# A retention layer and its gated feed-forward: order of the first loads, and the down-projection of the first chunk in thirds

## The chip, the cores and the metric

The kernel runs on one core of a Trainium2 chip. A time is that of the device for one execution, in microseconds (us); the figure for a kernel is the median of its runs.

## The reference, cut to what matters

Inputs are q, k, v of shape (4 batches, 8 heads, 768 positions, 64) and the feed-forward weights, all float32. The output has 3072 rows of 512.

```python
for t in range(S):                                   # S = 768, per batch and head
    state = gamma * state + outer(k[t], v[t])        # gamma = 1 - 2 ** (-5 - head)
    y[t] = scale * (q[t] @ state)
x = y.transpose(0, 2, 1, 3).reshape(B * S, H * D)    # 3072 x 512
xn = x / sqrt(mean(x * x) + 1e-6) * rms_g
out = (silu(xn @ w_gate) * (xn @ w_val)) @ w_out     # 512 -> 1536 -> 512
```

## The kernel before, in words

**Tiling.** The recurrence is computed in six chunks of 128 positions. Within a chunk, scores of q and k are taken on PE, masked by decay on DVE and multiplied with v; earlier chunks enter through a 64 x 64 state per head. The decay is folded into scalings of v and of the result. After that a chunk's 512 rows (4 batches x 128) are normed, transposed and put through the feed-forward: `gv` multiplies blocks of 128 gate and value columns (12 blocks) and leaves silu(gate) * value in `hT`; `down` multiplies `hT` with wo, 12 matmuls of 128x512 for each batch. Chunks 0 and 1 are worked in pairs of batches (pair 0: batches 0 and 1; pair 1: batches 2 and 3) with 64 partitions for each batch. In chunks 0 and 1 PE transposes q and k (`tp`, copied out by `tc_`), and chunk 0's masks hold the decay itself.

**Order.** The program is written out by hand: each engine carries out its instructions in the order of the text, from L568 on, and engines wait for one another by semaphores alone. What matters here is the head of the text, up to the first chunk's feed-forward, and three queues in it:

- POOL issues all transfers that convert float32 to bf16 (q, k and weights), and some of v. Its order: q and k of pair 0 (L124, L132), the index patterns `off` and `offp`, half of v of pair 0 (L136), q and k of pair 1 (L137, L138), the positions `pos_p`, `pos_n`, the exponents `ya_p` (L195), weight blocks 0 to 4 two at a time (L569, L570; `load_w` L83 is one transfer of wg and one of wv), the power for pair 0's norm (L603), blocks 4 to 8, the scaling of v (`vp_pair`), blocks 8 to 10, the power for pair 1 (L633), loads of chunk 1, blocks 10 to 12, wo in three parts (L652).
- SP issues the other half of v of pair 0 (L119) and, after the first masked score, v of pair 1 (L587).
- PE alternates pair 0's work, pair 1's transposes and scores, and `gv` blocks of pair 0 (columns 0 to 256 of the chunk), then pair 1's `y0`, its norm and transposes (`x_pe`, L644), then the rest of `gv`. `heat(n)` is n matmuls of ones whose result nobody reads.

The norm of chunk 0 (`squares0`, `eps0`, `power`, `norm0`) runs over ACT, DVE and POOL. `v_cast` (L267) makes a bf16 copy of v on ACT; `y0` needs it. `exponents` (L198) makes `va_p` and `va_n` on DVE from `pos_p` and `pos_n`.

**PSUM.** `bank` (L65) hands out the eight banks. First the list `first` (L59), then the cycle `order`; once `split[0]` is set, attention takes banks 0 to 3 in turn and the feed-forward 4 to 7. A new tile in a bank waits until the readers of the old one are through. Before, `split[0]` is set at L723, ahead of chunk 1's feed-forward.

**The first down-projection** (L682 to L709): `down(0, 0)` stands behind `y1(0)`, chunk 1's values of pair 0; `down(0, 1)` and `down(0, 2)` follow pair 0's norm; then come the transposes and scores of chunk 1, pair 1 (`tp`, `x_pe` of pair 0, `ap`), and `down(0, 3)`. Each copies its result to `o_sb` (three buffers) on ACT and stores it from SP's queue, on which the transposing loads of chunk 2 (`t_dma`) are queued too.

Of the kernel before, what the change touches and what calls it, by code (L numbers as in the profile page):

```python
# [8 lines left out]
F32 = mybir.dt.float32  # L9
# [7 lines left out]
def kernel(  # L17
# [11 lines left out]
    nc = tc.nc  # L29
    ctx.enter_context(tc.manual_schedule())  # L30

    B, H, S, D = q.shape
    C = 128
    NCH = S // C
    NHP = H // 2
    DM = H * D
    DFF = moe_w_gate.shape[1]
    KS = DM // 128
    NFF = DFF // 128
# [5 lines left out]
    work = ctx.enter_context(tc.tile_pool(name="work", bufs=4))  # L45
# [17 lines left out]
    split = [False]  # L63

    def bank(name, dtype=F32, ffn=False, i=None):  # L65
        if i is None and split[0]:
            i = turn[ffn] % 4 + 4 * ffn
            turn[ffn] += 1
        elif i is None and first:
            i = first.pop(0)  # L70
        elif i is None:
            i = order[0]
            order.append(order.pop(0))
        return psum.tile([128, 512 if dtype == F32 else 1024], dtype, name=name, tag=f"p{i}")
# [3 lines left out]
    wo_b = const.tile([128, NFF, DM], BF16, name="wo_b")  # L78
# [4 lines left out]
    def load_w(n0, n1, *kinds):  # L83
        sl = slice(n0 * 128, n1 * 128)
        for i in kinds or (0, 1):
            nc.gpsimd.dma_start(out=(wg_b, wv_b)[i][:, :, sl], in_=(wg_v, wv_v)[i][:, :, sl])
# [4 lines left out]
    U = {}  # L91

    def load_pair(c, p, n, batches=(0, 1), eng=None, after=None):
        u = U.setdefault((c, p), {})
        if n not in u:
            if n == "v":
                u[n] = work.tile([128, H, 2 * D], F32, name="v2f", bufs=3)
            else:
                u[n] = work.tile([128, H, 2 * D], BF16, name=n + "2b", bufs=4)
        for b in batches:  # L100
            i = (eng or nc.gpsimd).dma_start(out=u[n][b * 64:b * 64 + 64], in_=pair_v[n][c, 2 * p + b])  # L101
            if after is not None:
                tc.add_manual_dep(i.ins, after.ins.name, SYNC_DEP, reason="transfer order")
# [30 lines left out]
    for i in range(2):  # L134
        nc.gpsimd.iota(offp[i * 64:i * 64 + 64], pattern=[[-1, 2], [1, 2], [2, 64]], base=0, channel_multiplier=-2)
    load_pair(0, 0, "v", (1,))  # L136
    load_pair(0, 1, "q")  # L137
    load_pair(0, 1, "k")  # L138
    for i in range(2):
        nc.gpsimd.iota(pos_p[i * 64:i * 64 + 64], pattern=[[C, 2], [1, 2]], base=1, channel_multiplier=2,  # L140
                       allow_small_or_imprecise_dtypes=True)
# [36 lines left out]
    def mask_exp(a):  # L178
        for i in range(2):
            for x in range(2):  # L180
                nc.scalar.activation(mask0[a][i][:, x], reach, AF.Exp, scale=lng[2 * (2 * a + x) + i], bias=lnscale)
# [11 lines left out]
    for e in range(2):  # L193
        r = slice(e * 64, e * 64 + 64)
        nc.gpsimd.tensor_tensor(out=ya_p[r], in0=pos_p[r, 1, e:e + 1].to_broadcast([64, H]),  # L195
                                in1=lngs[r], op=ALU.mult)

    def exponents():  # L198
        nc.vector.tensor_tensor(
            out=va_p, in0=pos_p[:, :, None, :].to_broadcast([128, 2, H, 2]),  # L200
            in1=lngs[:, None, :, None].to_broadcast([128, 2, H, 2]), op=ALU.mult)
        nc.vector.tensor_tensor(
            out=va_n, in0=pos_n[:, :, None].to_broadcast([128, NCH, H]),
            in1=lngs[:, None, :].to_broadcast([128, NCH, H]), op=ALU.mult)
# [11 lines left out]
    def heat(n, i=7):  # L216
        hot = bank("hot", i=i)
        for _ in range(n):
            nc.tensor.matmul(hot, ones[:, :128], ones, start=True, stop=True)  # L219

    def copy(eng, out, in_):
        return (nc.scalar.copy if eng == "a" else nc.vector.tensor_copy)(out, in_)


    def tp(c, p, n, a, eng=None):

        u = U[c, p]
        ps = bank("t_ps", BF16)
        view = ps[:, :512].rearrange("p (x b e j) -> p x e b j", x=2, b=2, e=2)
        for x in range(2):  # L230
            for e in range(2):
                for i in range(2):
                    h = 2 * (2 * a + x) + i
                    nc.tensor.transpose(view[i * 64:i * 64 + 64, x, e], u[n][:, h, e * D:e * D + D], ident)  # L234
        u["t_ps", n, a] = ps
        if eng:
            tc_(c, p, n, a, eng)

    def tc_(c, p, n, a, eng):
        u = U[c, p]  # L240
        t = work.tile([128, 2, 2, 2, 64], BF16, name=n + "2T", tag=n + "T", bufs=8)
        copy(eng, t.rearrange("p x b e j -> p (x b e j)"), u["t_ps", n, a][:, :512])
        u[n + "T", a] = t
# [14 lines left out]
    def ap_mask(c, p, a, i):  # L258
        u = U[c, p]
        am = work.tile([128, 2, 2, 128], BF16, name="am2", tag="am", bufs=12)  # L260
        m = mask0[a][i] if c == 0 else causal_p[:, None, :].to_broadcast([128, 2, 256])
        u["mask", a, i] = nc.vector.tensor_tensor(  # L262
            out=am.rearrange("p x e t -> p x (e t)"),
            in0=u["a_ps", a][i].rearrange("p (x t) -> p x t", x=2), in1=m, op=ALU.mult)
        u["am", a, i] = am

    def v_cast(p):  # L267
        u = U[0, p]
        u["vb"] = work.tile([128, H, 2 * D], BF16, name="vb", bufs=2)
        nc.scalar.copy(u["vb"], u["v"])  # L270
# [87 lines left out]
    def begin(c):  # L358
        XT[c] = work.tile([128, KS, GT], BF16, name="xnT", bufs=2)
# [35 lines left out]
    def y1_out(p):  # L395
        u = U[1, p]
        x = work.tile([128, 2, NHP, 2, D], F32, name="x", tag="x", bufs=2)
        u["x"] = x.rearrange("p b a i d -> p b (a i d)")
        for b in range(2):
            nc.vector.tensor_tensor(  # L400
                out=u["x"][:, b].rearrange("p (h d) -> p h d", h=H), in0=u["y"][b].rearrange("p (h d) -> p h d", h=H),
                in1=yd_p[:, :, None].to_broadcast([128, H, D]), op=ALU.mult)
# [115 lines left out]
    HT = {}  # L518
# [22 lines left out]
    def store(eng, c, b, m, o_sb):  # L541
        if c < 2:
            for e in range(2):
                eng.dma_start(out=out_e[c, b, e][:, m], in_=o_sb[e * 64:e * 64 + 64, m])
        else:
            eng.dma_start(out=out_v[c, b][:, m], in_=o_sb[:, m])

    def down(c, b):
        ps = bank("o_ps", ffn=True)
        for n in range(NFF):  # L550
            nc.tensor.matmul(ps, HT[c][:, n, b * C:(b + 1) * C], wo_b[:, n, :], start=n == 0, stop=n == NFF - 1)  # L551
        o_sb = work.tile([128, DM], F32, name="o_sb", bufs=3)
        nc.scalar.copy(o_sb, ps)  # L553
        store(nc.sync, c, b, slice(0, DM), o_sb)

    def down_last(c, b):
        o_sb = work.tile([128, DM], F32, name="o_sb", bufs=3)
        for i in range(2):
            m = slice(i * 256, i * 256 + 256)
            ps = bank("o_ps", ffn=True)  # L560
            for n in range(NFF):
                nc.tensor.matmul(ps[:, :256], HT[c][:, n, b * C:(b + 1) * C], wo_b[:, n, m],  # L562
                                 start=n == 0, stop=n == NFF - 1)
            copy("av"[i], o_sb[:, m], ps[:, :256])
            store(nc.scalar if i == 0 else nc.sync, c, b, m, o_sb)


    begin(0)  # L568
    load_w(0, 2)  # L569
    load_w(2, 4)  # L570

    mask_exp(0)
    mask_exp(1)
    heat(11)
    tp(0, 0, "q", 0, "v")
    tp(0, 0, "q", 1, "v")
    heat(1)
    tp(0, 0, "k", 0, "v")
    tp(0, 0, "k", 1, "v")
    exponents()  # L580
    heat(2)
    ap(0, 0, 0)
    ap(0, 0, 1)
    for a in range(2):
        for i in range(2):
            ap_mask(0, 0, a, i)
    load_pair(0, 1, "v", eng=nc.sync, after=U[0, 0]["mask", 0, 0])  # L587
    v_cast(0)

    g_ps = bank("g_bc_ps")  # L590
# [6 lines left out]
    squares0(0)  # L597
    tp(0, 1, "q", 0, "a")
    tp(0, 1, "q", 1, "a")
    tp(0, 1, "k", 0)  # L600
    tp(0, 1, "k", 1)
    eps0(0)
    power(0, 0)  # L603
    tc_(0, 1, "k", 0, "v")
    tc_(0, 1, "k", 1, "v")
    load_w(4, 6)
    load_w(6, 8)
    vp_pair(0, 0)
# [70 lines left out]
    gv(0, 11, 12, 0, GT)  # L679
    load(2, 0)  # L680
    y1(0)
    down(0, 0)  # L682
    y1_out(0)
    square(1, 0, 0)
    square(1, 0, 1)
# [3 lines left out]
    load(2, 1)  # L689
    vp_pair(1, 1)  # L690
    load(2, 2)
    down(0, 1)
    down(0, 2)
    t_dma(2, 0)
    for n, e in (("q", "a"), ("k", "v")):
        for a in range(2):
# [9 lines left out]
            ap_mask(1, 1, a, i)  # L706
    load(2, 3)
    t_dma(2, 1)
    down(0, 3)  # L709

    def run(steps, after):
        for i, step in enumerate(steps):
# [4 lines left out]
    def L(f, *a):  # L717
        return lambda: f(*a)
# [1 line left out]

    steps = [L(gv, 1, n, n + 2, t, t + 256) for t in (0, 256) for n in range(0, NFF, 2)]
    steps += [L(down, 1, b) for b in range(B)]
    split[0] = True  # L723
    run(steps, {
        0: [L(y1, 1), L(y1_out, 1), L(kvp, 1, 1)],
        1: [L(square, 1, 1, 0), L(square, 1, 1, 1), L(rstd, 1, 1), L(state1, 1)],
# [18 lines left out]
    for c in range(2, NCH):  # L745
# [6 lines left out]
        after = {}  # L752
        if d < NCH:
            after = {
                0: [L(begin, d)],
                1: [L(values, d, 0), L(vp, d, 2), L(vp, d, 3)],
                2: [L(y_out, d, 0, 0)] + [L(load, d + 1, 0)] * more,
                3: [L(y_out, d, 0, 1)] + [L(state_add, d, 0)] * more,
                4: [L(square, d, 0, 0)] + [L(load, d + 1, 1)] * more,
                5: [L(a_pair, d, 1), L(a_mask, d, 2, 0), L(square, d, 0, 1), L(rstd, d, 0)]  # L760
                   + [L(state_cast, 0)] * more,
                6: [L(a_mask, d, 2, 1), L(norm, d, 0, 0), L(x_dma, d, 0, 0)]
# [40 lines left out]
```

## Time and profile before

| | us |
|---|---|
| median of 11 runs | 239.38 (238.43 to 241.1) |
| the profiled execution | 240.46 |
| its span in the profile | 238.7 |
| PE busy | 225.7 (95%) |
| DVE, POOL, ACT busy | 129.2, 115.7, 87.5 |

The profile is of one execution. "Busy" is time in which an instruction of the engine ran; PE's weight loads (PEld) overlap its matmuls. A row of a timeline has the start in the span, the length, the engine, the line, the operation, its tiles and shapes, the number of instructions merged, and in brackets the idle time before it with what ended it. The row of a stretch has its length and then, for PE, PEld, DVE, ACT and POOL, busy time and number of instructions; at its end stand the granted PE clock (1.00 is full), the share of the transfer engines and GB/s. The chain is followed back from the last instruction to whatever released each step; a row has start, length and the step.

### The profile page before, as it was taken

The page shows a single profiled execution, that of the slowest core. Times are in us where ns is not written, and L with a number is a line of the kernel's source. Part 1 is how long each engine was busy: PE and PEld are TensorE (multiplying, and loading weights), DVE is VectorE, ACT ScalarE, POOL GpSimd, SP SyncE. Part 2 cuts the span into 40 slices and gives each one's busy share as a digit, 9 for nine tenths or more (in the row PEclk, how much of TensorE's full clock was granted, in tenths as well). Part 3 has the DMA queues.
Part 4 walks back from the last instruction along what each step waited for, and adds up shares of the span by engine and source line. Part 5 has one row for each costly group of instructions (what it writes and reads, how often), then busy time and mean ns, then how long its engine had stood idle before and what let it go on. Part 6 is the DMA issues. An engine that isn't in the chain of part 4 may idle for free.

```text
span 238.7 us, 5411 instructions
## 1 busy us (share of the span) xinstructions
PE 225.7 (95%) x2198; PEld 137.3 (58%) x2223; DVE 129.2 (54%) x222; ACT 87.5 (37%) x176; POOL 115.7 (48%) x150
## 2 busy tenths in 40 slices
PE   6785999999999999999999999999999999999993
PEld 2453785545788865585454684444674444854443
DVE  3774735638676585837866346966245742243300
ACT  2954544333153244225424235323325241333221
POOL 8966599839869941981936902927001000000000
PEclk9999999999999999999999999999999999999999
DMA  8999999999999999599999993994510204200022
GB/s 106 162 190 200 152 165 162 195 205 201 189 145 178 199 160 175 102 179 132 89 133 179 103 174 124 110 190 109 156 56 0 44 3 141 79 3 0 0 88 89
DMA packets 83306, 30.24 MB, mean 127 GB/s; under 512 B 69521, under 2 KB 78993, under 8 KB 83282
## 3 DMA queue, kind: packets, MB, share of 16 engines
q0 software_dynamic: 51328, 16.52, 64.2%
q1 hardware_dynamic: 31280, 13.25, 27.7%
q8 instruction: 17, 0.28, 0.5%
q10 hardware_dynamic: 674, 0.14, 0.3%
q14 instruction: 7, 0.06, 0.1%
HBM read 28.32 MB, written 6.29 MB: 145 GB/s over the span
## 4 chain that ended last, share of the span: by engine, by line
PE 86%; DMA 6%; DVE 3%; POOL 2%; issue 2%; DVEq 0%; POOLq 0%
PE v_ps L532 25%; PE o_ps L551 25%; PE g_ps L532 24%; DMA wv_b<-in_moe_w_val_dram 4%; DMA k2b<-in_k_dram 2%; PE y_ps L505 2%; PE a_ps L460 2%; DVE am L262 1%; PE y_ps L489 1%; PE t_ps L234 1%; PE o_ps L562 1%; PE kv_ps L498 1%; PE a_ps L255 1%; PE x_ps L365 1%; POOL q2b L101 1%
## 5 line engine op out<-in xcount | busy, mean ns | idle before, releaser
L537 DVE TENSOR_TENSOR hT<-sg,v_ps 128x512 bf16<-128x512 bf16 (+1 forms) x76 | 49.8, 656 | 75.3 <-PE v_ps L532 72.9
L532 PE MATMUL v_ps<-xnT,wv_b 128*128 128x256 bf16 (+1 forms) x427 | 74.9, 309 | 2.3 <-DMA wv_b<-in_moe_w_val_dram 1.9
L532 PE MATMUL g_ps<-xnT,wg_b 128*128 128x256 bf16 (+1 forms) x415 | 73.5, 307 | 1.7 <-DMA wg_b<-in_moe_w_gate_dram 1.0
L536 ACT ACTIVATE sg<-g_ps 128x512 bf16<-128x512 f32 (+1 forms) x76 | 43.7, 574 | 81.8 <-PE g_ps L532 76.9
L551 PE MATMUL o_ps<-wo_b,hT 128*128 128x512 bf16 x268 | 60.8, 379 | 0.4
L532 PEld LDWEIGHTS <-wv_b 128*128 128x128 bf16 x428 | 41.6, 98 | 23.4 <-DMA wv_b<-in_moe_w_val_dram 2.8
L532 PEld LDWEIGHTS <-wg_b 128*128 128x128 bf16 x428 | 40.3, 98 | 21.2 <-DMA wg_b<-in_moe_w_gate_dram 1.3
L551 PEld LDWEIGHTS <-hT 128*128 128x128 bf16 x276 | 26.5, 98 | 31.4
L429 POOL TENSOR_SCALAR m<-ms 128x2 f32<-128x2 f32 x10 | 2.2, 219 | 68.8 <-ACT xsq L424 68.8
L553 ACT COPY o_sb<-o_ps 128x512 f32<-128x512 f32 x23 | 13.4, 582 | 43.7 <-PE o_ps L551 43.7
L437 DVE SCALAR_TENSOR_TENSOR xn<-x,rstd,g_bc 128x512 bf16<-128x512 f32 x20 | 21.9, 1122 | 12.9 <-POOL rstd L345 12.9
L469 DVE TENSOR_TENSOR am<-a_ps,causal 128x512 bf16<-128x512 f32 x32 | 20.8, 678 | 0.0
L443 POOL TENSOR_TENSOR vp<-v_f,vd_n 128x512 bf16<-128x512 f32 x16 | 20.1, 1277 | 0.0
L113 POOL DMA_DIRECT2D qb<-in_q_dram x16 | 15.0, 937 | 0.6 <-DMA wo_b<-in_moe_w_out_dram 0.6
L424 ACT ACTIVATE xsq<-x 128x512 bf16<-128x512 f32 x20 | 12.4, 623 | 7.7 <-DVE x L415 7.7
L113 POOL DMA_DIRECT2D kb<-in_k_dram x16 | 14.3, 896 | 1.8 <-DMA wo_b<-in_moe_w_out_dram 1.8
L110 POOL DMA_DIRECT2D v_f<-in_v_dram x16 | 14.7, 917 | 0.0
L415 DVE TENSOR_TENSOR x<-y_ps,yd_n 128x512 f32<-128x512 f32 x16 | 10.8, 682 | 0.6 <-PE y_ps L505 0.6
L219 PE MATMUL hot<-ones 128*128 128x512 bf16 x22 | 7.8, 457 | 1.5 <-DVE ones L146 1.4
L275 POOL TENSOR_TENSOR vp<-v2f,vd_p 128x1024 bf16<-128x1024 f32 x4 | 7.8, 1945 | 0.1
L345 POOL TENSOR_TENSOR rstd<-m,mhalf 128x2 f32<-128x2 f32 x10 | 7.2, 718 | 0.8
L101 POOL DMA_DIRECT2D q2b<-in_q_dram x8 | 5.8, 738 | 0.8 <-POOLq L787 0.8
(92 smaller groups left out, 154.6 us busy)
## 6 DMA issues: line engine op xcount, KB each, us to landing
v_f<-in_v_dram POOLq DMA_DIRECT2D x16, 256.0 KB, 7.7
out_dram<-o_sb SPq DMA_DIRECT2D x15, 256.0 KB, 2.3
out_dram<-o_sb SPq DMA_DIRECT2D x17, 128.0 KB, 4.4
qb<-in_q_dram POOLq DMA_DIRECT2D x16, 128.0 KB, 6.0
kb<-in_k_dram POOLq DMA_DIRECT2D x16, 128.0 KB, 7.2
wg_b<-in_moe_w_gate_dram POOLq DMA_DIRECT2D x6, 256.0 KB, 9.3
wv_b<-in_moe_w_val_dram POOLq DMA_DIRECT2D x6, 256.0 KB, 10.0
wo_b<-in_moe_w_out_dram POOLq DMA_DIRECT2D x3, 512.0 KB, 9.4
```

What stands on the lines that cost most here:

```text
L110: nc.gpsimd.dma_start(out=x, in_=unit_v[n][c, b])
L113: nc.gpsimd.dma_start(out=x.rearrange("p (h d) -> p h d", h=H), in_=unit_v[n][c, b])
L415: nc.vector.tensor_tensor(out=x[:, :, :, i, :], in0=u["y"][i].rearrange("p (b a d) -> p b a d", b=2, a=NHP), in1=yd_n[:, c, i][:, None, :, ...
L424: nc.scalar.activation(xsq, u["x"][:, b], AF.Square, scale=1.0 / math.sqrt(DM), accum_out=u["ms_"][:, b:b + 1])
L437: nc.vector.scalar_tensor_tensor(out=u["xn"][b], in0=u["x"][:, b], scalar=u["rstd"][:, b:b + 1], in1=g_bc, op0=ALU.mult, op1=ALU.mult)
L443: nc.gpsimd.tensor_tensor(out=x, in0=U[c, b]["v"], in1=vd_n[:, c, :, None].to_broadcast([128, H, D]), op=ALU.mult)
L469: nc.vector.tensor_tensor(out=x, in0=u["a_ps"][i].rearrange("p (a t) -> p a t", a=NHP), in1=causal[:, None, :].to_broadcast([128, NHP, 128 ...
L532: nc.tensor.matmul(x[:, o:o + w], wt[:, s, n * 128:(n + 1) * 128], XT[c][:, s, t0:t1], start=s == 0, stop=s == KS - 1)
L536: nc.scalar.activation(sg[:, :m], ps[0][:, :m], AF.Silu)
L537: return nc.vector.tensor_tensor(out=HT[c][:, n0:n1, t0:t1], in0=sg[:, :m].rearrange("p (n t) -> p n t", t=w), in1=ps[1][:, :m].rearrange( ...
L551: nc.tensor.matmul(ps, HT[c][:, n, b * C:(b + 1) * C], wo_b[:, n, :], start=n == 0, stop=n == NFF - 1)
L553: nc.scalar.copy(o_sb, ps)
```

## The change

Four edits, all of order. Weight block 0 alone is loaded ahead of pair 1's q and k, which move behind the positions and `ya_p`; block 1 and blocks 2 to 4 follow them. The load of v of pair 1 moves from SP's queue to POOL's, behind the first power. `exponents` moves ahead of the copies of the first k, one of pair 1's k copies goes from DVE to ACT, and the counts of `heat` change. The first chunk's down-projection is done in thirds of wo, for all four batches in turn, in four banks held at once, and `split[0]` is set ahead of it.

```diff
     load_pair(0, 0, "v", (1,))
-    load_pair(0, 1, "q")
-    load_pair(0, 1, "k")
+    load_w(0, 1)
     for i in range(2):
         nc.gpsimd.iota(pos_p[i * 64:i * 64 + 64], pattern=[[C, 2], [1, 2]], base=1, channel_multiplier=2,
...
                                 in1=lngs[r], op=ALU.mult)
+    load_pair(0, 1, "q")
+    load_pair(0, 1, "k")
+    load_w(1, 2)
+    load_w(2, 4)
...
+    DP = {}
+
+    def down_third(c, t, *bs):
+
+        for b in bs or range(B):
+            if t == 0:
+                DP[b] = bank("o_ps", ffn=True)
+            for n in range(4 * t, 4 * t + 4):
+                nc.tensor.matmul(DP[b], HT[c][:, n, b * C:(b + 1) * C], wo_b[:, n, :], start=n == 0, stop=n == NFF - 1)
+            if t == 2:
+                o_sb = work.tile([128, DM], F32, name="o_sb", bufs=3)
+                nc.scalar.copy(o_sb, DP[b])
+                store(nc.sync, c, b, slice(0, DM), o_sb)
...
     begin(0)
-    load_w(0, 2)
-    load_w(2, 4)
-
     mask_exp(0)
     mask_exp(1)
-    heat(11)
+    heat(12)
     tp(0, 0, "q", 0, "v")
     tp(0, 0, "q", 1, "v")
-    heat(1)
+    exponents()
+    heat(3)
     tp(0, 0, "k", 0, "v")
     tp(0, 0, "k", 1, "v")
-    exponents()
     heat(2)
...
-    load_pair(0, 1, "v", eng=nc.sync, after=U[0, 0]["mask", 0, 0])
     v_cast(0)
...
     tp(0, 1, "q", 1, "a")
+    heat(3)
     tp(0, 1, "k", 0)
     tp(0, 1, "k", 1)
     eps0(0)
     power(0, 0)
     tc_(0, 1, "k", 0, "v")
-    tc_(0, 1, "k", 1, "v")
+    tc_(0, 1, "k", 1, "a")
+    load_pair(0, 1, "v")
     load_w(4, 6)
     load_w(6, 8)
...
     y1(0)
-    down(0, 0)
+    split[0] = True
+    down_third(0, 0)
     y1_out(0)
...
-    down(0, 1)
-    down(0, 2)
+    down_third(0, 1)
+    down_third(0, 2, 0)
     t_dma(2, 0)
...
-    down(0, 3)
+    down_third(0, 2, 1, 2, 3)
...
     steps += [L(down, 1, b) for b in range(B)]
-    split[0] = True
```

## The prediction

> **What bounds the kernel now.** I read the page first: PE is busy 225.7 of 238.7 us, and of its forty slices only the first four and the last show less than 9 tenths. So I asked for the busy time by stretches.
>
> ```profile
> PE   6785999999999999999999999999999999999993
> ...
> 17.48:28.45 10.97, 7.85 (x115) 5.34 (x116) 6.50 (x15) 5.76 (x11) 5.98 (x8) 1.00 1.35 189
> 28.45:48.50 20.05, 19.79 (x278) 13.42 (x281) 10.50 (x20) 8.19 (x17) 18.14 (x23) 1.00 1.20 168
> 48.50:61.40 12.90, 12.76 (x121) 6.48 (x121) 8.54 (x13) 3.97 (x9) 9.82 (x12) 1.00 1.71 219
> ```
>
> First number after the stretch: its length; then PE's busy time. From 28.45 on PE idles 0.3 us in 20 and 0.1 in 13: what comes later moves one for one with the head, unless the change opens gaps there. Between the first feed-forward (gv) matmul (17.48) and the transposes of the second pair's normed rows (x_pe, 28.45) PE idles 3.1 us. PE's timeline of that stretch says why:
>
> ```profile
> 18.95 0.61 PE L532 MATMUL v_ps<-xnT,wv_b 128*128 128x256 bf16 x4 [0.88 <-DMA wv_b<-in_moe_w_val_dram]
> ...
> 21.45 0.61 PE L532 MATMUL g_ps<-xnT,wg_b 128*128 128x256 bf16 x4 [1.01 <-DMA wg_b<-in_moe_w_gate_dram]
> 23.11 0.61 PE L532 MATMUL v_ps<-xnT,wv_b 128*128 128x256 bf16 x4 [1.05 <-DMA wv_b<-in_moe_w_val_dram]
> ...
> 24.53 0.64 PE L290 MATMUL y_ps<-vb,am 64*128 64x64 bf16 x32
> ...
> 25.78 0.61 PE L532 MATMUL v_ps<-xnT,wv_b 128*128 128x256 bf16 x4
> ```
>
> Three waits for weights, 2.94 us. The chain agrees: one 9.60 us transfer fills it before 25.78.
>
> ```profile
> 15.41 0.73 POOL wg_b L86
> 16.14 9.60 DMA wv_b<-in_moe_w_val_dram
> ```
>
> Last, issue plus landing time, one transfer at a time (v2f, wg_b, wv_b, q2b, k2b in short windows). Second pair: q lands at 10.1 and 11.0, k at 11.8 and 12.5. Weights by two blocks (256 KB each): 14.8, 18.9, 21.4, 23.1, 24.4, 25.7, 27.1, 28.4. From 23.1 on the step is 1.34 us, before it up to 4.1. In between lies that pair's v (2 x 256 KB, from SP's queue): issued at 10.86 and 11.52, landed at 19.7 and 22.2, and ACT's cast of it ran at 22.32. So the stage is bound by transfers, and mixing the two queues is its slow part.
>
> **The change part by part.** *First block and POOL's queue.* A half block (128 KB, 256-byte rows) has its nearest row in q and k: 128 KB in 256-byte rows land every 0.75 to 0.87 us, against 0.67 for half of a 1.34 us step. Four halves cost 4 x 0.13 = 0.5 us of transfer (ends 0.3 and 0.8) and two more issues of 0.76 on POOL. POOL after its v issue (5.92): two halves to 7.45, iotas and the yield exponents 1.0 to 8.45, q and k (four of 0.69) to 11.2, four weight issues to 14.25. The power waits for DVE until 14.69 today: cover 0.44 us; without it each further issue would add 0.76 to the first norm.
>
> *Exponents.* DVE now waits for pos_n (about 8.1), 0.28 of work, done at 8.4; behind it queue the copies of kT, which start at 8.95 for k landed at 8.36. Cost nothing; cover 0.5.
>
> *Heat matmuls.* 12 for 11 lie ahead of a 0.95 wait, 3 for 1 ahead of a 1.23 wait; at 0.43 and 2 x 0.22 they fit. The new three before the second k's transposes lie in that k's wait, below.
>
> *Second q, k.* Issue to landing was 4.2 to 4.6 with this queue ahead, so q (issued 8.45 and 9.15) lands at 12.6 and 13.3, k at 14.0 and 14.7 to 15.0: 2.3 later. PE is in order: tp of k at 14.75 (13.43 before), its copies to 15.4 (DVE) and 15.95 (ACT, 0.53; this one now ahead of the first norm on ACT, 15.44 before), scores (ap) 16.05 to 16.7, heat 0.2, the first x_pe at 16.9 (16.18), first gv at 18.2 (17.48). Loss 0.7 (ends 0.4 and 1.1), covered if the next item ends later.
>
> *Second v on POOL's queue.* Here a rule speaks against the change. Issued at 10.86 from SP, v took 8.9 and 10.7 us; the first pair's second half, POOL-issued, took 4.2, landing 1.04 after the k before it. The Trainium skill, "DMA: Bandwidth & Descriptors", section "Issuing engine by pattern", has simple loads go from Sync and calls that path generally faster. By the rule, v from POOL would not land before today's 22.2, and POOL's two issues (1.4 us) would be pure cost; the head would gain nothing. By the rows I take another sum: once k has landed (14.7), halves 0.8 each: 15.5, 16.3; blocks of 1.34: 17.65, 19.0; v at 1.2 each, between 1.04 and the 1.35 of the next chunk's: 20.2, 21.5. Bound below: issue 16.1 + 4.2 = 20.3. Bound above: the rate of 14.8 to 22.2, 1 MB in 7.45 us = 141 KB/us, for everything after 14.7 (1.31 MB in 9.3): 24.0. I take 21.5, since the slow rate ends when SP's transfers end.
>
> *What is late next.* Weights no longer hold gv 0 to 3 (18.2 to 21.7). Then the cast of v: 21.5 + 1.05 = 22.6, so y0 of pair 1 starts at 22.65 (24.53). The cast stands on ACT ahead of two Silus, DVE's hT behind those and bn_stats behind hT: bn at 22.6 + 0.4 + 2 x 0.42 = 23.85 (25.24), x_pe 3.2 later as today: 27.05. The other arm: v_ps of block 4 needs its block, 1.34 x 2 after v, 24.2 (25.78), x_pe 2.67 later: 26.9. The head gains 28.45 - 27.05 = **1.4 us**; with v at 20.3 it gains 2.6, at 24.0 it loses 1.1. vp_pair and later loads on POOL shift by 1.4 for the two v issues and sat 5 us before the second power: hidden.
>
> *Down-projection by thirds.* As many matmuls (48) and copies. The last wo third lands at 49.1, wanted at 50.2 today; with loads and PE both moved up, the thirds save nothing (at most 0.3 of PE's gain). Their price is the banks: four are held, and `split` leaves four to attention. Today:
>
> ```profile
> 56.34 0.64 PE L234 MATMUL t_ps<-ident,q2b 128*64 128x128 bf16 x16
> 56.81 0.61 PE L234 MATMUL t_ps<-ident,k2b 128*64 128x128 bf16 x16
> 57.35 0.83 PE L365 MATMUL x_ps<-ident,xn 128*128 128x128 bf16 x8
> 58.12 0.75 PE L255 MATMUL a_ps<-q2T,k2T 64*64 64x128 bf16 x32
> 58.80 2.76 PE L551 MATMUL o_ps<-wo_b,hT 128*128 128x512 bf16 x11
> ```
>
> From the first transpose to the next o_ps: 2.46 us. In the new order the first x_pe takes the bank of the first transposed q, which ACT frees after the o_sb copy (0.58) and its own (0.53): 1.3 after the start instead of 1.0; the second x_pe waits for the next copy (1.85), and the second scores for DVE's copy of x_ps (2.75). Sum 3.05: **+0.6 us** (ends 0 and 0.9). Stores of three batches move behind the chunk-2 transposes on SP; these start earlier for it, and nothing waits for a store but the fourth o_sb.
>
> **Sum.** -1.4 + 0.6 = -0.8. The profiled execution took 240.46 (span 238.7 and 1.8 around it): 239.7. The median of the runs is 1.1 below it: 239.38 - 0.8 = 238.6.
>
> **Rivals.** *Rates stay mixed* (the other side): v queued behind six weight transfers moves at 141 KB/us whichever queue it is in. It lands at 24.0, head +1.1, banks +0.6: 241.1. It breaks even at v = 22.4 and decides for slower by 0.5% at 23.6. For it: the step from 14.8 to 18.9. Against: 1.34 us steps right after, and v from POOL at 1.04. *All of the head*: v lands near its bound (20.3 to 20.8) and bank waits hide behind the transposes' own: 2.1 to 2.6 less 0 to 0.3, 237.1. For it: PE's own work would allow y0 at 21.7. Against: four weight transfers are ahead. *Does nothing*: the wait on weights turns into one on v's cast or on k, of the same length; head 0, banks 0 to 0.6: 239.7. The profile excludes it only if v lands before 22.
>
> **How the numbers follow.** Measurement tells 0.5% (1.2 us) from no change. Forecast 0.48, its own range 237.9 to 239.3; all of the head 0.27; nothing 0.08; mixed rates 0.17. Faster by over 0.5% (below 238.2): all of the head and a fourth of the forecast, 0.39. Slower (above 240.6): most of mixed rates, 0.15. Within: 0.46. Range 236.9 to 240.5: it leaves out most of mixed rates and the tail of the second case.
>
> **What would show it.** Right: no PE wait on wg_b or wv_b in blocks 0 to 3; q and k transposes of pair 1 up to 1.3 us later, first gv near 18.2; v landed near 21.5, cast at once, and PE waiting about 0.9 us ahead of y0 for it; x_pe of pair 1 near 27.05; 3.0 us from tp(1,1) to the next o_ps, with waits by ACT and DVE copies. Wrong: v landed after 22.4; the first power on POOL starting after 14.7, because issues took over 0.76; a wait on wo_b inside the thirds; or new PE gaps after the thirds, where I count none.

## The result, and the profile after

The changed kernel takes 243.08 us (median of 12 runs, 241.08 to 249.9), the kernel before 239.41 in the 47 runs made beside it. The ratio is 1.0117, with a 95% interval of 1.0089 to 1.0144: slower by 2.1 to 3.4 us, above the forecast of 238.6 and above the range, which ended at 240.5. Runs that a disturbance of the chip lengthened are in the medians here, and out of every ratio.

The profiled execution took 241.38 us, with a span of 239.2; 2.2 us lie outside the span, where before's had 1.8 (the means over all runs are 2.11 and 1.78). Its busy tenths and its stretches, cut at the same places as those of before (length, then busy time and number of instructions of PE, PEld, DVE, ACT and POOL, granted clock, share of the transfer engines, GB/s):

```profile
PE   7777899999999999999999999999999999999993
...
17.48:28.45 10.97, 8.79 (x147) 6.50 (x137) 7.09 (x16) 6.31 (x13) 7.43 (x10) 1.00 1.37 203
28.45:48.50 20.05, 19.79 (x278) 13.43 (x281) 10.65 (x20) 8.19 (x17) 18.23 (x23) 1.00 1.26 178
48.50:61.40 12.90, 12.31 (x116) 6.38 (x118) 7.14 (x13) 3.70 (x9) 11.58 (x14) 1.00 1.65 191
```

From 17.48 to 28.45 PE is busier by 0.9 us, 28.45 to 48.50 is unchanged, and the stretch with the down-projection has lost 0.45 us. PE's timeline of the changed kernel's head:

```profile
13.75 0.64 PE L237 MATMUL t_ps<-ident,q2b 128*64 128x128 bf16 x16 [0.60 <-DMA q2b<-in_q_dram]
...
15.78 0.64 PE L237 MATMUL t_ps<-ident,k2b 128*64 128x128 bf16 x16 [0.65 <-DMA k2b<-in_k_dram]
...
19.19 0.60 PE L535 MATMUL g_ps<-xnT,wg_b 128*128 128x256 bf16 x4 [0.24 <-ACT xnT L225]
...
24.40 0.64 PE L293 MATMUL y_ps<-vb,am 64*128 64x64 bf16 x32 [1.56 <-ACT vb L273]
...
25.42 0.60 PE L535 MATMUL v_ps<-xnT,wv_b 128*128 128x256 bf16 x4
...
28.35 0.65 PE L368 MATMUL x_ps<-ident,xn 128*128 128x128 bf16 x8 [0.32 <-ACT xn L355]
```

No wait on weights is left in blocks 0 to 3. One wait of 1.56 us for v's cast stands in its place, and the second pair's x_pe comes at 28.35, against 28.45 in the profile of before. By these two profiles alone the head has gained a tenth of a microsecond. The chain of the changed kernel says what fills it:

```profile
15.53 0.69 POOL v2f L101
16.22 7.07 DMA v2f<-in_v_dram
23.28 0.02 issue
23.31 1.04 ACT vb L273
```

And PE's timeline around the thirds, with the waits that the prediction announced: 3.20 us from the first transpose to the next o_ps (2.46 before, 3.05 predicted).

```profile
56.27 0.64 PE L237 MATMUL t_ps<-ident,q2b 128*64 128x128 bf16 x16
56.74 0.61 PE L237 MATMUL t_ps<-ident,k2b 128*64 128x128 bf16 x16
...
57.51 0.87 PE L368 MATMUL x_ps<-ident,xn 128*128 128x128 bf16 x8
58.31 1.00 PE L258 MATMUL a_ps<-q2T,k2T 64*64 64x128 bf16 x32
...
59.47 0.81 PE L567 MATMUL o_ps<-wo_b,hT 128*128 128x512 bf16 x3 [0.16 <-issue]
```

The waits are those: x_pe starts when ACT has copied the first transposed q, and the second scores when DVE has copied x_ps. So the two traces show 0.1 us gained in the head and 0.7 lost at the banks (3.20 less 2.46), and not where 2.8 us come from.

### The profile page after: what moved, and what is told of

It reads as the page before. It is cut to its first block, busy times and chain, and to the rows that moved or that the text cites. A ratio compares the mean times of both kernels' runs of the same rounds, so it can differ in the third digit from the quotient of the medians.

```text
span 239.2 us, 5420 instructions
## 1 busy us (share of the span) xinstructions
PE 226.6 (95%) x2204; PEld 138.3 (58%) x2229; DVE 127.7 (53%) x221; ACT 88.1 (37%) x177; POOL 118.6 (50%) x154
## 4 chain that ended last, share of the span: by engine, by line
PE 84%; DMA 5%; DVE 4%; POOL 2%; issue 2%; ACT 2%; DVEq 0%; POOLq 0%
PE v_ps L535 25%; PE g_ps L535 24%; PE o_ps L554 21%; PE o_ps L567 4%; DMA v2f<-in_v_dram 3%; DMA k2b<-in_k_dram 2%; PE y_ps L508 2%; PE a_ps L463 2%; DVE am L265 1%; PE y_ps L492 1%; PE o_ps L579 1%; PE kv_ps L501 1%; DVE hT L540 1%; PE t_ps L237 1%; POOL q2b L101 1%
## 5 line engine op out<-in xcount | busy, mean ns | idle before, releaser
L440 DVE SCALAR_TENSOR_TENSOR xn<-x,rstd,g_bc 128x512 bf16<-128x512 f32 x20 | 20.2, 1038 | 11.2 <-POOL rstd L348 11.2
L556 ACT COPY o_sb<-o_ps 128x512 f32<-128x512 f32 x19 | 11.0, 581 | 33.0 <-PE o_ps L554 33.0
L110 POOL DMA_DIRECT2D v_f<-in_v_dram x16 | 14.7, 919 | 0.0
L222 PE MATMUL hot<-ones 128*128 128x512 bf16 x28 | 9.4, 444 | 1.5 <-DVE ones L145 1.4
```

The costliest lines, as they stand in the source:

```text
L110: nc.gpsimd.dma_start(out=x, in_=unit_v[n][c, b])
L440: nc.vector.scalar_tensor_tensor(out=u["xn"][b], in0=u["x"][:, b], scalar=u["rstd"][:, b:b + 1], in1=g_bc, op0=ALU.mult, op1=ALU.mult)
```

## The experiments

**The theories.** *Clock* (A in the expectations): many runs of the changed kernel show a granted clock below 1.00, so gaps in the new head cost PE its clock. *Thirds* (B): the banks account for all of it. *Bytes* (C): up to x_pe of the second pair the head is bound by what has to be moved before v, or before the value weights of blocks 4 and 5 (wv of blocks 4 to 6, for short); the order of the bytes decides little. *Mixing* (D: it slows; F: it helps): it matters whether v runs on SP's queue beside POOL's. *Late issue* (E): microseconds in which POOL's queue is not yet filled are lost for good. Where a span is given below, it is the median over the runs at full granted clock (a mean of 0.996 or more over the execution): 237.6 to 237.7 for the kernel before, 239.1 for the changed one, which had three such runs.

**The head by itself, the thirds by themselves, and the clock.** The head: the changed kernel with the old down-projection.

```diff
-    split[0] = True
-    down_third(0, 0)
+    down(0, 0)
...
-    down_third(0, 1)
-    down_third(0, 2, 0)
+    down(0, 1)
+    down(0, 2)
...
-    down_third(0, 2, 1, 2, 3)
+    down(0, 3)
...
+    split[0] = True
```

> The changed head with the down-projection of before. Theory A (the head makes the PE clock drop in many executions, and that is most of the loss): mean granted clock below 0.995 in most runs, 1.5 to 2.5 us slower than before in the median, though the profiled span at full clock is within 0.3 us of before. Theory B (the loss is bank waits in the thirds): same time as before within 0.3 us.

Measured: 1.0069 (1.0042 to 1.0097), span 238.8 at full clock, in seven of its ten runs. The head is not a gain, it is a loss of 1.2 us in the span, and it is one at full clock.

The thirds: the kernel before with `down_third` and `split[0]` as in the change.

```diff
-    down(0, 0)
+    split[0] = True
+    down_third(0, 0)
...
-    down(0, 1)
-    down(0, 2)
+    down_third(0, 1)
+    down_third(0, 2, 0)
...
-    down(0, 3)
+    down_third(0, 2, 1, 2, 3)
...
-    split[0] = True
```

> The head of before, the down-projection in thirds. Theory A: clock as before, about 0.6 us slower (bank waits at the transposes of chunk 1, pair 1). Theory B: 1.5 to 2.8 us slower, all of the change's loss.

Measured: 1.0026 (1.0000 to 1.0052), span 238.2: the +0.6 us that the prediction gave the banks. As the whole of the loss, *thirds* falls.

The clock: the changed kernel with seven more heat matmuls, into PSUM bank 2, in the gap ahead of y0.

```diff
+    heat(7, 2)
     y0(1, 0)
```

> The changed kernel with seven heat matmuls (7 x 0.216 = 1.5 us) in the wait ahead of the second pair's y0. Theory A: the granted clock stays at 1.00 in most runs and the median comes down by 1.5 to 2 us, to about 0.5 to 1 us above before. Theory B: no difference from the changed kernel, since the heat fills a wait that is there anyway.

Measured: 1.0101 (1.0070 to 1.0132). The four runs behind the ratio had a clock of 0.997 or more, and a span of 240.15, not below the changed kernel's 239.1. PE's timeline (of an execution with a span of 247.6, which lost its time from 61 to 100 us) shows the gap filled, y0 at the same time, and a wait behind it:

```profile
22.81 1.67 PE L222 MATMUL hot<-ones 128*128 128x512 bf16 x7
24.42 0.64 PE L293 MATMUL y_ps<-vb,am 64*128 64x64 bf16 x32
...
26.91 0.61 PE L535 MATMUL v_ps<-xnT,wv_b 128*128 128x256 bf16 x4 [1.30 <-DMA wv_b<-in_moe_w_val_dram]
```

With the clock kept up the loss is still there, and so it is in the head by itself: as most of the loss, *clock* falls. What a full clock is worth to the changed kernel can't be read from these four runs, since wv landed at 26.86 in this profile, 1.5 us later than in the changed kernel's, and x_pe came at 29.58; the sum at the end comes back to it. Stretches at half clock do occur in the heads of several of these kernels (3.4 us in the next one's profile); the four profiles used here that have one are 0.4 to 1.3 us longer than their kernel's median span at full clock. The kernel before has such runs too.

**v ahead of blocks 2 to 4.** In the changed kernel, the second pair's v and those blocks trade places.

```diff
     load_w(1, 2)
-    load_w(2, 4)
+    load_pair(0, 1, "v")
...
-    load_pair(0, 1, "v")
+    load_w(2, 4)
     load_w(4, 6)
```

> The changed kernel with the second pair's v issued ahead of weight blocks 2 to 4 (those now behind the first power). v lands near 19 instead of 23.3, so the 1.56 us wait ahead of y0 goes; the next limit is PE itself or weight block 2. Theory A and B both expect x_pe of the second pair 1.0 to 1.6 us earlier in the profile; A expects the clock to hold besides, so 2.5 to 3.5 us faster than the changed kernel; B expects 1.0 to 1.6 us.

Measured: 1.0064 (1.0035 to 1.0092), span 238.75, only 0.35 below the changed kernel's. The wait for v is gone, yet x_pe came only at 28.11 (with the half clock from 13.6 to 17.0 in this profile): wv of blocks 4 to 6 landed at 25.39, as in the changed kernel (25.37). With v early, the other arm of the prediction's sum binds. That speaks for *bytes*.

**The kernel before once more.** Unchanged, for a second profile.

> The kernel before, unchanged, for a second profile. In the profile shown, its execution took 240.46, 1.1 above its own median; the runs at full clock have spans near 237.4 instead of 238.7. If its usual head is about 1.2 us shorter than the one I read, x_pe of the second pair comes at 27.1 to 27.4 instead of 28.45, and the loss of the changed head (1.4 us in span) is measured against that. If the head is the same, the 1.2 us must lie behind it.

Measured: 0.9991 (0.9969 to 1.0013), and in its profiled execution (238.88 us, span 237.1) PE's timeline reads:

```profile
19.86 0.61 PE L532 MATMUL g_ps<-xnT,wg_b 128*128 128x256 bf16 x4 [0.70 <-DMA wg_b<-in_moe_w_gate_dram]
...
21.35 0.61 PE L532 MATMUL v_ps<-xnT,wv_b 128*128 128x256 bf16 x4 [0.88 <-DMA wv_b<-in_moe_w_val_dram]
...
22.77 0.64 PE L290 MATMUL y_ps<-vb,am 64*128 64x64 bf16 x32
...
26.70 0.61 PE L365 MATMUL x_ps<-ident,xn 128*128 128x128 bf16 x8
```

and its chain

```profile
15.91 8.07 DMA wv_b<-in_moe_w_val_dram
24.03 0.61 PE v_ps L532 x4
```

This decides half of the case. x_pe comes at 26.70, 1.75 us earlier than in the profile that the prediction worked from, and the same transfer of wv takes 8.07 us where that profile had 9.60. Now take x_pe from the span: what follows it lasted 210.25 us in the first profile (238.7 - 28.45) and 210.4 in the second (237.1 - 26.70). So the whole difference between the two executions lies ahead of x_pe. The same subtraction gives 210.1 to 210.5 in the profiles at full clock of eight other kernels here that have the old down-projection, and 210.85 in the changed one. The kernel before has a median span of 237.6, hence a usual x_pe at 237.6 - 210.3 = 27.3; the changed one, with 239.1, has it at 28.25. The head loses about 1 us, and does not gain 0.1.

**Which part of the head.** The first blocks and everything else of the new head, with v back on SP and the old down-projection:

```diff
+    load_pair(0, 1, "v", eng=nc.sync, after=U[0, 0]["mask", 0, 0])
     v_cast(0)
...
-    load_pair(0, 1, "v")
```

> The changed head without the move of v (v from SP again, after the first masked score), down-projection of before. Theory A (v behind six weight transfers on POOL's queue is what makes the head slower): as before within 0.4 us. Theory B (the later q and k hold PE up, in order, and v is only the next wait): 1.0 to 1.6 us slower than before, like the whole head. Either way the time outside the span shows whether this edit adds the 0.35 us there (2.1 in place of 1.8).

Measured: 1.0043 (1.0021 to 1.0065), span 238.1 and 1.94 outside it.

The kernel before, with v on POOL behind the first power:

```diff
-    load_pair(0, 1, "v", eng=nc.sync, after=U[0, 0]["mask", 0, 0])
...
     tc_(0, 1, "k", 1, "v")
+    load_pair(0, 1, "v")
     load_w(4, 6)
```

> The kernel before with only v of the second pair moved to POOL's queue, behind the first power. Theory A: v lands after the four weight transfers of before and later than 22.2, near 22 to 23; 0.8 to 1.5 us slower than before. Theory B: v lands by 21.5 since the queues no longer mix, and the kernel is as before or up to 1 us faster.

Measured: 1.0032 (1.0009 to 1.0056), span 238.4. v landed at 22.50, later than the 20.23 of the unchanged kernel's second profile, and PE waits for it:

```profile
23.67 0.64 PE L290 MATMUL y_ps<-vb,am 64*128 64x64 bf16 x32 [2.28 <-ACT vb L270]
...
27.61 0.63 PE L365 MATMUL x_ps<-ident,xn 128*128 128x128 bf16 x8 [0.32 <-ACT xn L352]
```

The same move the other way: v on POOL too, but right behind the second q and k and ahead of all weights.

```diff
+    load_pair(0, 1, "v")
     load_w(0, 2)
...
-    load_pair(0, 1, "v", eng=nc.sync, after=U[0, 0]["mask", 0, 0])
```

> The kernel before with v of the second pair issued by POOL straight after that pair's q and k, ahead of all weights. Theory C (the head is bound by the bytes that must land by weight block 6, whatever their order: that block's wv landed at 25.4 to 25.7 in all of before, changed, and the kernel with v ahead of blocks 2 to 4): wv of blocks 4 to 6 lands at 25.4 again and the time is as before within 0.4 us. Theory D (mixing SP's queue with POOL's is what slows the transfers): it lands near 23, no PE wait for weights, and 1 to 2 us faster than before.

Measured: 238.86 us, 0.9972 (0.9946 to 0.9998), span 236.9: the only kernel here with all of the work whose interval lies below 1, if barely. v landed at 15.1. Two waits on weights stay, and x_pe comes earlier than in any other profile of a kernel with all of the work:

```profile
18.53 0.61 PE L532 MATMUL v_ps<-xnT,wv_b 128*128 128x256 bf16 x4 [0.40 <-DMA wv_b<-in_moe_w_val_dram]
...
21.20 0.61 PE L532 MATMUL v_ps<-xnT,wv_b 128*128 128x256 bf16 x4 [0.73 <-DMA wv_b<-in_moe_w_val_dram]
...
26.55 0.61 PE L365 MATMUL x_ps<-ident,xn 128*128 128x128 bf16 x8
```

Between the last two kernels only the place of v in POOL's queue differs, and they lie 0.6% apart. With v late, wv of blocks 4 to 6 lands at 24.57, and 2.7 later, at 27.3, x_pe could have started, as in a usual execution of before; it starts 0.3 later, for v. With v first wv lands at 23.83 with just as many bytes ahead of it, and v is off the path. Neither expectation came true as it stood: *bytes* had wv at 25.4 and the time as before, *mixing slows* had 1 to 2 us.

The first two blocks as halves, nothing else:

```diff
-    load_w(0, 2)
+    load_w(0, 1)
+    load_w(1, 2)
```

> The kernel before with its first two-block weight load cut into two single blocks (256-byte rows instead of 512), nothing moved. Theory C (bytes and their row size bound the head): stretches with 256-byte rows moved 130 to 150 KB per us, those with 512-byte rows 195, so the 512 KB cost 3.6 us instead of 2.6: wv of block 5 lands 0.8 to 1.2 later and the kernel is 0.8 to 1.2 us slower. Rival (the halves cost only the 0.5 of the prediction, and the loss comes from the order, the late k): 0 to 0.5 us slower.

Measured: 1.0024 (0.9993 to 1.0055), span 237.5 and 1.94 outside it; half clock from 21.3 to 24.7 in its profile. In the span the halves by themselves cost nothing that shows. Inconclusive for the total.

**Thirds with x_pe ahead of the transposes.** The kernel before with the thirds, and `x_pe` and `x_copy` of pair 0 moved ahead of the loop of `tp` and `tc_` for chunk 1, pair 1, so that x_pe no longer takes over a bank that the transposes have just filled.

```diff
-    for n, e in (("q", "a"), ("k", "v")):
-        for a in range(2):
-            tp(1, 1, n, a, e)
     x_pe(1, 0, 0)
     x_copy(1, 0, 0, "v")
     x_pe(1, 0, 1)
     x_copy(1, 0, 1, "v")
+    for n, e in (("q", "a"), ("k", "v")):
+        for a in range(2):
+            tp(1, 1, n, a, e)
```

> The kernel before with the down-projection in thirds, and the x_pe of chunk 1, pair 0 with its copies put ahead of the transposes of pair 1. Theory (the thirds' loss is the bank that x_pe takes over from the transposed q, freed late by ACT): the waits by ACT copies (0.15 and 0.11 us) and by DVE's x_ps copy (0.12) go, the stretch from the first transposes to the next o_ps is 2.5 instead of 3.0 us, and the kernel is as before within 0.3 us. Rival (the thirds lose elsewhere, in stores or late chunk-2 transposes): 0.5 to 0.7 us slower, like the thirds alone.

Measured: 1.0019 (0.9996 to 1.0043), span 237.95 against 238.2 for the thirds as they are. PE's timeline:

```profile
54.97 0.61 PE L365 MATMUL x_ps<-ident,xn 128*128 128x128 bf16 x8
55.51 0.64 PE L234 MATMUL t_ps<-ident,q2b 128*64 128x128 bf16 x16
55.98 0.64 PE L234 MATMUL t_ps<-ident,k2b 128*64 128x128 bf16 x16
...
56.89 0.84 PE L255 MATMUL a_ps<-q2T,k2T 64*64 64x128 bf16 x32 [0.28 <-DVE k2T L222]
57.66 2.76 PE L564 MATMUL o_ps<-wo_b,hT 128*128 128x512 bf16 x12
```

(The execution has a span of 243.8; what it lost lies at 100 to 150 us, where PE is busy 46.3 of 50.) From the first transpose to the next o_ps it is 2.15 us, with x_pe's 0.54 moved ahead of it 2.69: between before's 2.46 and the change's 3.20. The takeover of banks is the price of the thirds. The two totals alone do not tell these kernels apart.

**The rest of the head.** The kernel before with the positions ahead of the second q and k, the exponents early, the new heat counts, and one k copy on ACT.

```diff
-    load_pair(0, 1, "q")
-    load_pair(0, 1, "k")
...
     nc.gpsimd.iota(pos_n, pattern=[[C, NCH]], base=1, channel_multiplier=1,
                    allow_small_or_imprecise_dtypes=True)
+    load_pair(0, 1, "q")
+    load_pair(0, 1, "k")
...
-    heat(11)
+    heat(12)
...
-    heat(1)
+    exponents()
+    heat(3)
...
-    exponents()
...
+    heat(3)
...
-    tc_(0, 1, "k", 1, "v")
+    tc_(0, 1, "k", 1, "a")
```

> The kernel before with only the small edits of the changed head: positions made ahead of the second q and k, exponents ahead of the first k's copies, the heat counts, and the k copy on ACT; weights and v as before. Theory C: transfers in the same order and rows, so as before within 0.4 us in span. Rival: these edits cost 0.5 us or more by themselves, in span or in the 0.35 us outside it (2.1 in place of 1.8).

Measured: 1.0028 (1.0011 to 1.0045), span 238.5 in 19 runs. A part whose edits the prediction had at nothing, but for the delay of q and k, costs 0.7 us. In its profile wv of blocks 4 to 6 landed at 25.56, and x_pe came at 28.27.

**No second v.** The kernel before without that load: the first pair's v stands in for it, so that chunk 0 of batches 2 and 3 is computed from the wrong v.

```diff
-    load_pair(0, 1, "v", eng=nc.sync, after=U[0, 0]["mask", 0, 0])
+    U[0, 1]["v"] = U[0, 0]["v"]
```

> The kernel before without the load of the second pair's v: the first pair's v stands in for it, so chunk 0 of batches 2 and 3 is computed from the wrong v, with the same work on all engines and 512 KB less to move. Theory C: 512 KB at 195 KB per us is 2.6 us, so wv of block 5 lands near 21.4 instead of 24.0 and x_pe of the second pair comes 1.5 to 2.2 us earlier, at 24.5 to 25.2, where PE and the norm's chain bind. Rival (the head is bound by the order of waits, not by the bytes): under 0.7 us faster.

Measured: 0.9936 (0.9912 to 0.9960), span 235.9. With 512 KB less to move x_pe comes at 25.43, and it waits on weights as ever:

```profile
22.76 0.61 PE L532 MATMUL v_ps<-xnT,wv_b 128*128 128x256 bf16 x4 [0.47 <-DMA wv_b<-in_moe_w_val_dram]
...
25.43 0.61 PE L365 MATMUL x_ps<-ident,xn 128*128 128x128 bf16 x8
```

The first half of *bytes* stands: the stage is bound by transfers, and fewer of them give 1.7 us. The second half, that their order decides little, does not: the place of v alone makes 0.6%.

**Which part of the rest.** The positions ahead of the second q and k, by themselves. It moves these four issues 0.58 us down POOL's queue, and nothing else.

```diff
-    load_pair(0, 1, "q")
-    load_pair(0, 1, "k")
     for i in range(2):
         nc.gpsimd.iota(pos_p[i * 64:i * 64 + 64], pattern=[[C, 2], [1, 2]], base=1, channel_multiplier=2,
...
     nc.gpsimd.iota(pos_n, pattern=[[C, NCH]], base=1, channel_multiplier=1,
                    allow_small_or_imprecise_dtypes=True)
+    load_pair(0, 1, "q")
+    load_pair(0, 1, "k")
```

> The kernel before with the positions made ahead of the issue of the second q and k, nothing else: that issue comes 0.55 us later on POOL. Theory E (the transfer engines lose what POOL issues late, since POOL's queue runs dry behind the first v): the small edits' 0.7 us are here, 0.4 to 0.8 us slower. Rival (the heats and the k copy on ACT are what costs): as before within 0.2 us.

Measured: 1.0029 (1.0008 to 1.0051), span 238.1. POOL's timeline of this kernel, and PE's:

```profile
5.24 0.70 POOL L101 DMA_DIRECT2D v2f<-in_v_dram  x1
...
6.49 1.38 POOL L101 DMA_DIRECT2D q2b<-in_q_dram  x2
```

```profile
27.76 0.61 PE L365 MATMUL x_ps<-ident,xn 128*128 128x128 bf16 x8
```

In the unchanged kernel's second profile the q issues begin at 5.91. Their 0.58 us come back as 0.5 in the span, with x_pe 0.46 behind the usual 27.3 in this profile. From 8 to 12 us this kernel moves 132 GB/s, and the eight profiles with the old places of these issues and of v 141 to 151. *Late issue* stands.

The heat counts and the k copy on ACT, by themselves:

```diff
-    heat(11)
+    heat(12)
...
-    heat(1)
+    heat(3)
...
+    heat(3)
...
-    tc_(0, 1, "k", 1, "v")
+    tc_(0, 1, "k", 1, "a")
```

> The kernel before with the changed heat counts (12, 3 and the new 3) and one second k copy on ACT, transfers untouched. Theory E: as before within 0.2 us. Rival: the three heats ahead of the second k's transposes (0.65 us) and the copy ahead of the norm on ACT hold up the first gv, 0.4 to 0.8 us slower.

Measured: 0.9984 (0.9959 to 1.0009), span 237.7: nothing, as predicted.

**v earlier, but on SP.** v of the second pair issued from SP after the first copy of k, or after the first copy of q, where before it waits for the first masked score (`u` keeps the copies under new names).

```diff
-    load_pair(0, 1, "v", eng=nc.sync, after=U[0, 0]["mask", 0, 0])
+    load_pair(0, 1, "v", eng=nc.sync, after=U[0, 0]["kc", 0])
```

> The kernel before with v of the second pair still on SP's queue, but issued after the first k copy (9.3) instead of after the first masked score (10.7). Theory F (256-byte rows leave the transfer engines short, about 145 KB per us against 195 to 205 when a second queue or longer rows are in the mix, so v is best moved beside q and k): the stretch 10 to 14 us moves 30 to 60 KB per us more, wv of block 5 lands 0.4 to 1.0 us earlier and the kernel is 0.3 to 1.0 us faster. Rival (mixing only shifts the share between queues): q and k of the second pair land later by what v takes, and the kernel is as before or slower.

Measured: 0.9993 (0.9972 to 1.0014), span 237.5; v landed at 18.1, wv of blocks 4 to 6 at 23.86.

```diff
-    load_pair(0, 1, "v", eng=nc.sync, after=U[0, 0]["mask", 0, 0])
+    load_pair(0, 1, "v", eng=nc.sync, after=U[0, 0]["qc", 0])
```

> As the kernel with v on SP's queue after the first k copy, but after the first q copy (near 7.0). Theory F: 0.5 to 1.3 us faster than before, unless the first k (landing 8.36) is held up by it; then up to 0.5 us of that goes. Rival: as before or slower, with the first k later.

Measured: 0.9998 (0.9976 to 1.0020). In the profiled execution (span 241.8) the clock is halved from 12.9 to 23.1 us, and nothing is read from it. The eight runs at full clock have a span of 236.7, 0.9 below before and as low as with v first; the other eleven behind the ratio have clocks of 0.976 to 0.993 and a median span of 238.5, and take it back. So v beside weights does not slow the stage (*mixing slows* falls). Whether *mixing helps* stays open: 237.5 and 236.7 at full clock, no gain in either ratio, and with v first the same gain in the span comes from POOL's queue alone.

## Why the prediction was wrong, step by step

**The sum's base.** The step that failed first: "The profiled execution took 240.46 (span 238.7 and 1.8 around it): 239.7. The median of the runs is 1.1 below it". The 1.1 us came off at the end as a constant, after the late transfer that made them had been counted as the change's gain. The head's gain was put at 28.45 - 27.05 = 1.4 us. From the usual x_pe, 27.3, the same forecast gives 0.25, and with the banks' 0.6 the sum is 0.35 us above before: no change, even if every other step had held. A third profile with the old head (thirds with x_pe first) has x_pe at 27.18.

**The two arms were right.** x_pe is the later of two arms in each of these heads. Weights bind before: wv of blocks 4 to 6 lands at 23.98 and x_pe follows 2.72 us later; 25.73 and 2.72 in the first profile; 23.83 and 2.72 with v first; 25.04 and 2.72 with the positions ahead. v binds after the change: 23.28 and 5.07 (with v alone 22.50 and 5.11). The prediction had 2.67 and 5.55. In the changed kernel the two arms are close: its wv of blocks 4 to 6 landed at 25.37 (v_ps at 25.42), which by itself puts x_pe at 28.1, against 28.35 for v.

**v at 21.5, and the weights behind it at 24.2.** They landed at 23.28 and 25.37. That is the second failed step, worth 1.3 us at x_pe (28.35 for 27.05), and it is not v's alone: had v alone come at 21.5, the weights at 25.37 would have held x_pe to 28.1. The kernel with v ahead of blocks 2 to 4 shows it, with 28.11. Half of v's delay is k's: 15.65 and not 14.7, although its issue was on time. From k to v it was then 7.63 us and not 6.8: 0.4 more in the first half block, 0.5 in the last of the weights ahead. The unit costs (0.8 a half, 1.34 a chunk, 1.2 a v) were the best steps of the old trace, not its mean. The stretches show it, for the second profile of before and for the changed kernel:

```profile
8.00:12.00 4.00, 3.70 (x70) 1.85 (x70) 3.06 (x8) 3.99 (x11) 3.76 (x10) 1.00 1.45 145
12.00:16.00 4.00, 3.54 (x86) 2.13 (x86) 3.07 (x8) 2.56 (x6) 2.29 (x5) 1.00 1.23 181
16.00:20.00 4.00, 3.06 (x28) 2.17 (x29) 2.95 (x6) 2.53 (x4) 4.00 (x5) 1.00 1.34 208
```

```profile
8.00:12.00 4.00, 3.37 (x69) 1.85 (x70) 2.81 (x7) 3.62 (x10) 3.92 (x9) 1.00 1.31 135
12.00:16.00 4.00, 2.46 (x44) 1.28 (x45) 2.01 (x6) 2.39 (x6) 3.43 (x6) 1.00 1.54 146
16.00:20.00 4.00, 3.71 (x68) 2.39 (x65) 2.76 (x5) 2.61 (x4) 4.00 (x7) 1.00 1.34 202
```

The last column has 10, 35 and 6 GB/s less, 204 KB over the 12 us, which take 1.0 us at 202 GB/s. The prediction's reading of the old trace, "mixing the two queues is its slow part", was wrong: from 16 to 20 us, with v and weights under way together, before moves 208 GB/s. Steps of up to 4.1 us between landings are the order in which mixed transfers finish, not a rate.

Why the changed kernel moves 146 from 12 to 16 us stays open. Its halves, like q and k, have 256-byte rows, and the Trainium skill, "DMA: Bandwidth & Descriptors", section "Specifications", asks for 512 bytes or more for full rate. By that rule the halves would be the cause; but the halves alone have 180 GB/s in this stretch, and the rest of the head, without halves, has 140. The five profiles with the whole new head or its blocks have 138 to 153. Among heads that are the same the figure varies too (185, 181 and 182 in three profiles of the old one, 158 in a fourth with half clock there), so that one profile doesn't settle it.

**Costs put at nothing.** "q (issued 8.45 and 9.15)" was on time, and its price of 0.7 us was called "covered if the next item ends later". The positions alone show otherwise: 0.58 us of issue on POOL cost 0.3%, in a stage that is bound by transfers. The delay was weighed for the transposes of k, and not for the bytes behind them.

**Transposes of k and the first gv.** 15.78 and 19.19, predicted 14.75 and 18.2; late by k's landing, and then covered by the wait for v.

**The thirds.** Right in mechanism and size: +0.6 predicted; 3.20 us for 3.05 in the trace, 0.6 in the span when done alone, and 0.6 behind x_pe in the changed kernel (210.85 less 210.25). No wait on wo_b, as said.

**The slower rival** had v at 24.0, "head +1.1" and 241.1 in all. It is the nearest to what came, with v at 23.28 and about +1 us in the head; but its break-even at 22.4 was measured from 28.45 too, and its mechanism, mixed rates, was not the one: from k to v the changed kernel moved the 1.31 MB in 7.63 us, 172 KB/us and not 141.

**The sum as measured.** Head by itself 1.2 us in the span (238.8 less 237.6), banks 0.6, outside the span 0.33 (2.11 less 1.78, in every kernel with the whole new head): 2.1 us, or 0.9%; by the two ratios, 0.69% and 0.26%, together 0.95%. The head's 0.69% is that of v on POOL, 0.32%, and of everything else in it, 0.43%. From the prediction: 238.6, plus 1.15 for the base (27.3 for 28.45), 1.2 for the transfers (x_pe at 28.25 for 27.05) and 0.33, makes 241.3, and the changed kernel's three runs at full clock have a median of 241.17, 1.8 us above before's 239.4 at full clock.

The measured interval is 0.89 to 1.44%, with its middle at 2.8 us, and what it has above this lies in runs at a lower clock. Of the eight runs behind the ratio five have a clock of 0.983 to 0.993, and a median span of 240.9 where the three have 239.1. The kernel before has such runs too (238.3 to 238.9 for 237.6), but they are only 20 to 31% of its runs made beside the experiments. So about 1 us of the measured loss comes in with these runs. Whether the change makes such runs more frequent stays open: with the head alone they were three of ten, with the thirds alone nine of fourteen, with the added heat none of four. Open as well is what the 0.33 us outside the span are: the halves alone and the blocks with the rest show 0.16 of them, v alone and the rest alone none.

## What to carry to other kernels

Where the one profiled execution lies above its median, find the stage in which the excess lies before anything is taken off in that stage; a second profile of the same kernel was worth more here than a finer sum on the first. Where a stage is bound by transfers, an operand's place in the queue should follow the time at which it is wanted together with the work behind it (v needs 5.1 us to x_pe, weights 2.7, so v goes first), and an issue slot given away at the front is paid for at the end (0.5 us for 0.58 here). Take a rate from bytes per stretch, and not from the steps between landings.

## What the runs showed of the hardware that was not expected

- The new head lengthened the time outside the profiled span from 1.78 to 2.11 us; why was not settled.
- The same program's head differs by 1.75 us between two profiled executions at full clock (x_pe at 28.45 and 26.70), with the landing of one transfer (25.73 and 23.98). What delayed it was not found.
- A load of v from POOL took 4.3 and 4.8 us to land ahead of the weights, 5.3 to 7.1 behind them (v alone, and the changed kernel); from SP with the weights in flight 7.2 and 8.9 in before's second profile, 8.9 and 10.7 in its first. Its place in the order changed the time by more than its queue did.
- Half clock set in without a long pause of PE: in the profile of the halves alone PE was busy 1.72 of the 3.45 us ahead of it (17.8 to 21.25), with no wait over 0.73 us.
